# A fused sparse attention and MLP kernel: instruction order from a scheduling model with DMA limits as traced

## The chip, the cores and the metric

The kernel runs on one core of one Trainium2 chip. The metric is the device time of one execution in microseconds (us), as the median of several runs. The profile is of one execution. Its engines are PE (TensorE), ACT (ScalarE), DVE (VectorE), POOL (GpSimd) and SP (SyncE, which here issues transfers only); PEld is TensorE's weight load.

## What is computed

Attention over 4 batches, 8 heads, 768 positions and a head size of 64, in which each query sees only 6 of 24 chunks of 32 keys; then an MLP with an ELU over the 3072 resulting rows. The reference, cut to what matters:

```python
# q, k, v: (4, 8, 768, 64) float32; chunk = 32; top_k = 6; scale = 1/sqrt(64)
k_min, k_max = k_chunks.min(axis=3), k_chunks.max(axis=3)          # per chunk of 32 keys
ub = sum_d maximum(q * k_min, q * k_max)                           # bound per query and chunk
ub = where(causal, ub, -1e9)
top_chunks = argsort(ub)[..., -top_k:]
scores = scale * q @ k.T, masked to the chosen chunks and to earlier positions
attn = softmax(scores)
x = (attn @ v) as (3072, 512)
h = x @ w_in                                                       # w_in (512, 2048)
g = where(h > 0, h, exp(minimum(h, 0)) - 1)                        # ELU
out = g @ w_out                                                    # w_out (2048, 512)
```

## The kernel before

The kernel is written as a graph of operations. Each names the engines that could do it with a cost on each, the buffers that it reads and writes, and a priority. When the program is built, a simulated run of this graph on the five engines decides which engine does what and in which order, and which of a class's buffers each operation gets. The instructions are then emitted in that order. On the chip each engine works through its own fixed list, so an instruction whose data is late holds up all that stand behind it on its engine. The costs in the graph are used only for building; nothing of the model runs on the chip.

The work is cut into eight parts i = (b, h): batch b and half h of 384 positions. Each part has four head pairs r. For each pair, `prep` loads K, Q and V, transposes K and Q on PE and forms the chunk bounds; `select` makes the mask for two pairs; `attend` does scores, exponentials, attention times V, and the transposed result `xt`. `mlp(i)` needs the four `xt` of its part.

The parameters, which a search has set (numbers of buffers per class, gates of the weight loads, and offsets of priorities):

```python
T = dict(kf=6, qf=5, vf=7, pt=12, xt=12, gT=26, qt=3, qr=3, rhs=5, nfirst=2, vlate=4.17,
         gate=[1, 2, 3, 4, 5, 5, 8, 11], attw=[10.3, 19.0], mlp=[14.0, 15.1], loada=18.12,
         prepa=9.74, sela=2.41, fill=50)
```

The transfers in the model: each of the three queues (SP, ACT, POOL) works at one transfer at a time, and the queues that are busy share the bandwidth equally.

```python
def run(self, at=None, dma_lat=(700.0, 1300.0)):
    ...
    rings = {e: [] for e in (SP, ACT, POOL)}
    ...
    def transfer(t):
        ...
            live = [r for r in rings.values() if r and r[0][0] <= dma_at]
            ...
            if live:
                stop = min(stop, dma_at + min(r[0][1] for r in live) * len(live))
                for r in live:
                    r[0][1] -= (stop - dma_at) / len(live)
            ...
                    o.finish = dma_at + dma_lat[1]
```

The loads of a pair: two heads each of K, Q and V, 96 KB per transfer, in runs of 256 bytes (64 float32 of one position). All go on SP's queue but four Q loads at the start. Those of the first `nfirst` pairs come before everything else; V is later than K and Q by `vlate` in priority.

```python
for buf, src, late in ((kf, k, 0.0), (qf, q, 0.001), (vf, v, T["vlate"])):
    for hd in range(2):
        early = first and src is not v
        dma(..., (-100.0 + r) if early else prio + late, 450.0, ..., eng=ACT if early and late else SP)   # L411
```

The weights: four parts each of `w_in` and `w_out`, converted from float32 to bfloat16 in the transfer, issued by POOL. Each may be issued only once a certain number of V tiles has been cast to bfloat16 on POOL (L522); those numbers are `gate`.

```python
g.op(f"w_in{i}", c_dma(POOL, 900.0),
     lambda e: nc.gpsimd.dma_start(out=w_in_sb[:, :, 512 * i:512 * (i + 1)], in_=...),      # L364; w_out: L371
     writes=[(fixed, ("wi", i))], prio=-1.0, xfer=3400.0,
     after=[casts[W_GATE[i] - 1]] if W_GATE[i] else [])
```

TensorE's work by lines of the kernel: L454 transposes K and Q (float32, three blocks each); L540 multiplies queries with the chunk bounds; L606 scores; L662 attention times V; L687 transposes the result; L704 the first product of the MLP (per chunk fc four matmuls of 384 columns); L731 the second (per token tile tt and quarter c four matmuls of 512 columns):

```python
for fc in range(NFC):                       # 16
    pr = mlp_prio(i, 0.6 * fc / NFC)
    ... h: 4 matmuls (PE), e: exp (ACT, L712), m: e - 1 (POOL, L716), gT: min(max(h, 0), m) (DVE, L720)
for tt in range(3):
    for c in range(4):
        pr = mlp_prio(i, 0.6 + 0.4 * (tt * 4 + c) / 12)
        ... reads gts[4c : 4c + 4]
    ... copy to SBUF (L739), store
```

One tile `gT` holds one chunk fc of a part, so a part needs 16 of them until its last token tile has read them. Matmuls on zeros fill TensorE where the model has it idle, at the lowest priority:

```python
last = None
for i in range(T["fill"]):
    def fill(e, bank=bank):
        for _ in range(2):
            nc.tensor.matmul(ap(bank), lhsT=zeros[:, 0:P], rhs=zeros, start=True, stop=True)   # L762
    last = g.op("fill", {PE: (432, 600)}, fill, writes=[(bank, 0)], prio=1e6,
                after=[last] if last else [])
```

Of the kernel before, what the change touches and what calls it, by code (L numbers as in the profile page):

```python
# [29 lines left out]
NFC = DFF // P  # L30
# [7 lines left out]
SEM = 45.0  # L38


T = dict(kf=6, qf=5, vf=7, pt=12, xt=12, gT=26, qt=3, qr=3, rhs=5, nfirst=2, vlate=4.17,
         gate=[1, 2, 3, 4, 5, 5, 8, 11], attw=[10.3, 19.0], mlp=[14.0, 15.1], loada=18.12,
         prepa=9.74, sela=2.41, fill=50)


class Buf:
# [19 lines left out]
class Graph:  # L66
# [38 lines left out]
        self.ops.append(o)  # L105
        return o

    def run(self, at=None, dma_lat=(700.0, 1300.0)):
        free = {n: [(0.0, s) for s in range(len(v))] for n, v in self.slots.items()}
        engines = (PE, ACT, DVE, POOL, SP)  # L110
        at = {e: (at or {}).get(e, 0.0) for e in engines}
# [1 line left out]
        events = sorted({0.0, *at.values()})  # L113
        arriving = []
        rings = {e: [] for e in (SP, ACT, POOL)}
        dma_at, asked = 0.0, -1.0
        port_free = {DVE: 0.0, POOL: 0.0}
        for o in self.ops:
# [24 lines left out]
        def transfer(t):  # L143
            nonlocal dma_at, asked
            if asked <= t:
                asked = -1.0
            while True:
                live = [r for r in rings.values() if r and r[0][0] <= dma_at]
                later = [r[0][0] for r in rings.values() if r and r[0][0] > dma_at]
                stop = min([t] + later)  # L150
                if live:
                    stop = min(stop, dma_at + min(r[0][1] for r in live) * len(live))
                    for r in live:
                        r[0][1] -= (stop - dma_at) / len(live)
                dma_at = stop
                for r in live:
                    if r[0][1] <= 1e-6:
                        o = r.pop(0)[2]
                        o.finish = dma_at + dma_lat[1]
                        settle(o)  # L160
                if dma_at >= t:
                    break
            live = [r for r in rings.values() if r]
            if live:
                due = max(t, min(r[0][0] for r in live)) + min(r[0][1] for r in live) + 1.0
                if not due - 40.0 < asked <= due + 40.0:
                    asked = due
                    heapq.heappush(events, due)

        while left or any(rings.values()):  # L170
            if not events:
                held = {n: len(v) for n, v in free.items()}
                stuck = [o.name for e in engines for _, _, o in avail[e]][:40]
                raise RuntimeError(f"stuck: {left} left, free {held}, {stuck}")
            t = heapq.heappop(events)
            while events and events[0] <= t:
                heapq.heappop(events)
            transfer(t)
            while arriving and arriving[0][0] <= t:
                _, _, o = heapq.heappop(arriving)  # L180
                for e in o.engines:
                    bisect.insort(avail[e], (o.prio, o.seq, o))
            moved = True
            while moved:
                moved = False
                for e in engines:
                    if at[e] > t:
                        continue
                    lst = avail[e]
                    pick = None  # L190
                    i = 0
                    while i < len(lst):
                        o = lst[i][2]
                        if o.start is not None:
                            lst.pop(i)
                            continue
                        ok = True
                        for b in o.bufs:
                            if b.slot is None:
                                if not any(ft <= t for ft, _ in free[b.cls]):  # L200
                                    ok = False
                                    break
                            elif b.cls == "bank" and any(x != e and ft > t for x, ft in b.used.items()):
                                ok = False
                                break
                        if ok:
                            pick = o
                            lst.pop(i)
                            break
                        i += 1  # L210
                    if pick is None:
                        continue
                    o = pick
                    dur, lat = o.engines[e]
                    o.engine, o.start = e, t
                    if e == POOL or (e == DVE and o.port):
                        held = max(0.0, port_free[DVE if e == POOL else POOL] - t)
                        dur, lat = dur + held, lat + held
                        port_free[e] = t + dur
                    at[e] = t + dur  # L220
                    heapq.heappush(events, at[e])
                    for b in o.bufs:
                        if b.slot is None:
                            fl = free[b.cls]
                            k = min((ft, s, j) for j, (ft, s) in enumerate(fl) if ft <= t)[2]
                            b.slot = fl.pop(k)[1]
                    if o.xfer is None:
                        o.finish = t + lat
                        settle(o)
                    else:  # L230
                        rings[e].append([t + dur + dma_lat[0], o.xfer, o])
                        heapq.heappush(events, t + dur + dma_lat[0] + o.xfer)
                    order.append(o)
                    left -= 1
                    moved = True
# [30 lines left out]
def kernel(  # L266
# [95 lines left out]
    def load_w_in(i):  # L362
        g.op(f"w_in{i}", c_dma(POOL, 900.0),
             lambda e: nc.gpsimd.dma_start(out=w_in_sb[:, :, 512 * i:512 * (i + 1)],  # L364
                                           in_=wi[:, :, 512 * i:512 * (i + 1)]),
             writes=[(fixed, ("wi", i))], prio=-1.0, xfer=3400.0,
             after=[casts[W_GATE[i] - 1]] if W_GATE[i] else [])

    def load_w_out(i):
        g.op(f"w_out{i}", c_dma(POOL, 900.0),  # L370
             lambda e: nc.gpsimd.dma_start(out=w_out_sb[:, 4 * i:4 * i + 4, :],  # L371
                                           in_=wo[:, 4 * i:4 * i + 4, :]),
             writes=[(fixed, ("wo", i))], prio=-1.0, xfer=3400.0,
             after=[casts[W_GATE[4 + i] - 1]] if W_GATE[4 + i] else [])


# [28 lines left out]
    g.op("table", {ACT: (1300, 1300)}, lambda e: nc.scalar.activation(out=warm, in_=warm, func=AF.Exp),  # L405
         prio=-90.0)

    def dma(dst_src, writes, reads, prio, xfer, name, eng=SP, issue=490.0):
        def emit(e):
            d, s_ = dst_src()  # L410
            (nc.scalar if e == ACT else nc.sync).dma_start(out=d, in_=s_)  # L411
# [15 lines left out]
    def prep(b, h, r, prio):  # L427
        kf, qf, vf = load(b, h, r, prio - LOADAHEAD)
        tag = f"{b}{h}{r}"
        if h == 0:  # L430
# [3 lines left out]
            if b < 2:  # L434
                def ec(e, lb=lb):
# [4 lines left out]
                    else:  # L440
# [1 line left out]
                            out=ap(lb)[hi].rearrange("p h s -> p (h s)"),  # L442
                            in_=econst[hi].rearrange("p h c w -> p (h c w)"))
                g.op("ec" + tag, {DVE: (480, 560)}, ec, writes=[(lb, "e")], port=True,
                     prio=prio + 0.5, after=[ecs[-2]] if len(ecs) > 1 else [])
        lb = lhs[b, r]
        rb = rhs[b, h, r] = g.buf(f"rhs{h}")
        kst = ks[b, r]
# [33 lines left out]
        put("kt", lambda: ap(kt), lambda: ap(bank)[:, 0:HS], c_both(HS), [(bank, 0)], [(kt, 0)], prio)  # L482
        for hd, rows in enumerate((lo, hi)):
            put("ka", lambda hd=hd: ap(lb)[lo, hd, ts], lambda rows=rows: ap(kt)[rows],
                {DVE: (175, 260), POOL: (500, 560)}, [(kt, 0)], [(lb, (h, hd))], prio + 0.5)

        def sub(e):
            eng = nc.vector if e == DVE else nc.gpsimd
# [26 lines left out]
             reads=[(qt, 0)], writes=[(qr, 0)], prio=prio, port=True)  # L515
        for hd, rows in enumerate((lo, hi)):
            put("qa", lambda hd=hd: ap(rb)[lo, hd], lambda rows=rows: ap(qt)[rows],
                {DVE: (275, 360), POOL: (500, 560), ACT: (386, 480)}, [(qt, 0)], [(rb, hd)], prio + 0.5)

        casts.append(g.op(  # L520
            "v" + tag, {POOL: (520, 580)},
# [68 lines left out]
    def attend(b, h, r, prio, w):  # L590
# [2 lines left out]
        ls, rs = lhs[b, r], rhs[b, h, r]  # L593
        nst = len(steps[h])
        for si, segs in enumerate(steps[h]):
            pr = prio + w * 0.8 * si / nst
            wtot = max(pc + wd for (_k, _c, wd, pc) in segs)
            pt = g.buf("pt")
            both = wtot <= 256
# [47 lines left out]
                     port=True)  # L647
            for (kb, c0, wd, pc) in segs:
                seg[kb] = (pt, pc - (c0 - HS * h))
        pr = prio + w * 0.8  # L650
        o3 = g.buf("bank")

        def o3v():
# [41 lines left out]
    def mlp(i):  # L695
        b, h = divmod(i, 2)
        gts = []
        for fc in range(NFC):
            pr = mlp_prio(i, 0.6 * fc / NFC)
            bank = g.buf("bank")  # L700

            def mm1(e, bank=bank, fc=fc):
# [21 lines left out]
        for tt in range(3):  # L724
            bank, ob = g.buf("bank"), g.buf("o")
            for c in range(4):
                pr = mlp_prio(i, 0.6 + 0.4 * (tt * 4 + c) / 12)

                def mm2(e, bank=bank, c=c, tt=tt):
                    for fc in range(4 * c, 4 * c + 4):  # L730
# [16 lines left out]
    for i in range(2 * B):  # L747
# [5 lines left out]
            select(b, h, gr, att_prio(i, 0.5 * gr) - PREPAHEAD + T["sela"])  # L753
        for r in range(NPAIR):
            attend(b, h, r, att_prio(i, 0.25 * r), 0.25 * w)
    last = None
    for i in range(T["fill"]):
        bank = g.buf("bank")

        def fill(e, bank=bank):  # L760
            for _ in range(2):
                nc.tensor.matmul(ap(bank), lhsT=zeros[:, 0:P], rhs=zeros, start=True, stop=True)  # L762
        last = g.op("fill", {PE: (432, 600)}, fill, writes=[(bank, 0)], prio=1e6,
                    after=[last] if last else [])
    for i in range(4):
        load_w_in(i)
    for i in range(4):
# [40 lines left out]
```

## Time and profile before

| | before |
|---|---|
| median of 3 runs | 309.26 us (306.78 to 311.76) |
| span of the profiled execution | 308.6 us, clock 0.994 |
| read from memory, written | 27.26 MB, 6.29 MB |
| transfers on SP's queue | 64 of K, 60 of Q, 64 of V, 24 stores |
| transfers on POOL's queue | 4 of w_in, 4 of w_out, 512 KB each as written |

How to read it: busy time is the time in which an engine has at least one instruction running, as a share of the span. Strips have 40 slices of 7.7 us, each digit the busy share in tenths. The chain of waits is followed back from the last instruction; what stands on it sets the end. A timeline's line gives start, duration, engine, line, operation, what it writes and reads, how many; in brackets the idle time of the engine before it, and what ended that. Matmuls overlap in the profile, so their single durations add up to more than the time they take; the step from one to the next is what counts. A line number is that of the kernel before.

### The profile page before, as it was taken

How to read it: one execution, taken by the hardware profiler on the slowest of the kernel's cores; microseconds unless marked ns; L12 is line 12 of the kernel's file. 1: busy time of each engine (PE TensorE's matmuls, PEld its weight loads, DVE VectorE, ACT ScalarE, POOL GpSimd, SP SyncE). 2: the span in 40 equal slices, each digit the busy share in tenths (PEclk: the TensorE clock that was granted, in tenths of full speed). 3: DMA queues.
4: the chain of work that ended last, by engine and by line, in shares of the span. 5: the costliest groups of instructions: out<-in, count | busy, mean ns of one | idle time of the engine just before them, and what ended most of it. 6: DMA issues, size and time to landing. Idle time of an engine off the chain costs nothing.

```text
span 308.6 us, 6957 instructions
## 1 busy us (share of the span) xinstructions
PE 295.0 (96%) x2346; PEld 178.3 (58%) x2372; DVE 221.6 (72%) x676; ACT 204.2 (66%) x449; POOL 143.5 (46%) x309
## 2 busy tenths in 40 slices
PE   8965599999999999999999999999999999999998
PEld 3533355666566555765665565765665556655643
DVE  8953748998789947986799846894889649722820
ACT  2843328996599466967587748995698668853720
POOL 7845335675368414763466214661266124411710
PEclk9999979999999999999999999999999999999999
DMA  8999979979876514223332222230100010001002
GB/s 168 170 212 216 190 170 167 186 172 183 197 211 140 118 72 111 51 53 87 85 88 51 54 93 62 52 80 34 70 1 2 0 70 35 2 34 51 20 2 102
DMA packets 84515, 29.82 MB, mean 97 GB/s; under 512 B 77312, under 2 KB 81408, under 8 KB 84480
## 3 DMA queue, kind: packets, MB, share of 16 engines
q1 hardware_dynamic: 78656, 24.79, 33.1%
q0 software_dynamic: 4224, 4.19, 8.9%
q10 hardware_dynamic: 1600, 0.39, 0.6%
q8 instruction: 19, 0.31, 0.4%
q14 instruction: 16, 0.13, 0.2%
HBM read 27.26 MB, written 6.29 MB: 109 GB/s over the span
## 4 chain that ended last, share of the span: by engine, by line
PE 87%; DMA 7%; SPq 5%; issue 1%
PE bank L704 27%; PE bank L731 26%; PE bank L606 11%; PE bank L662 7%; PE bank L454 6%; PE bank L540 6%; SPq L411 5%; DMA qf<-in_q_dram 4%; DMA kf<-in_k_dram 3%; PE bank L762 2%; PE bank L687 2%
## 5 line engine op out<-in xcount | busy, mean ns | idle before, releaser
L704 PE MATMUL bank<-xt,w_in_sb 128*128 128x384 bf16 x512 | 95.8, 326 | 0.0
L716 POOL TENSOR_SCALAR m<-e 128x384 f32<-128x384 f32 x128 | 66.3, 524 | 58.2 <-ACT e L712 49.1
L731 PE MATMUL bank<-w_out_sb,gT 128*128 128x512 bf16 x362 | 92.0, 379 | 1.2 <-issue 0.2
L618 ACT ACTIVATE pt<-bank 128x384 bf16<-128x384 f32 (+1 forms) x160 | 76.6, 538 | 18.3 <-PE bank L606 18.0
L720 DVE SCALAR_TENSOR_TENSOR gT<-bank,m 128x384 bf16<-128x384 f32 x128 | 68.3, 547 | 13.1 <-POOL m L716 11.5
L712 ACT ACTIVATE e<-bank 128x384 f32<-128x384 f32 x128 | 61.8, 503 | 12.0 <-PE bank L704 9.8
L704 PEld LDWEIGHTS <-w_in_sb 128*128 128x128 bf16 x512 | 48.7, 98 | 28.6 <-issue 0.6
L464 POOL COPY lhs<-kt 64x384 bf16<-64x384 bf16 x62 | 32.7, 527 | 60.1 <-ACT kt L460 58.1
L731 PEld LDWEIGHTS <-gT 128*128 128x128 bf16 x384 | 35.9, 98 | 32.5 <-issue 0.6
L606 PE MATMUL bank<-rhs,lhs 128*128 128x384 bf16 (+2 forms) x288 | 54.4, 290 | 0.1
L606 PEld LDWEIGHTS <-lhs 128*128 128x128 bf16 x288 | 25.8, 98 | 19.0 <-issue 1.7
L474 DVE TENSOR_REDUCE kmm<-bank 128x12 f32<-128x384 f32 x64 | 33.2, 544 | 1.4 <-ACT kt L460 1.2
L739 ACT ACTIVATE o<-bank 128x512 f32<-128x512 f32 x23 | 13.7, 595 | 30.5 <-PE bank L731 28.9
L460 ACT ACTIVATE kt<-bank 128x384 bf16<-128x384 f32 x32 | 15.8, 494 | 23.6 <-PE bank L454 22.8
L460 ACT ACTIVATE rhs<-qt 64x384 bf16<-64x384 f32 x51 | 26.7, 523 | 4.3 <-DVE qt L462 3.5
L662 PEld LDWEIGHTS <-pt 128*128 128x128 bf16 x672 | 24.6, 99 | 8.1 <-issue 4.7
L762 PE MATMUL bank<-zeros 128*128 128x512 bf16 x96 | 26.9, 410 | 1.4 <-DVE warm L336 1.3
L633 DVE TENSOR_TENSOR pt<-pt,tri 128x512 bf16<-128x512 bf16 x32 | 15.4, 481 | 17.5 <-ACT pt L618 17.4
L662 PE MATMUL bank<-vext,pt 128*128 128x65 bf16 x672 | 26.6, 195 | 0.0
L454 PE MATMUL bank<-ident_f,kf 128*128 128x128 f32 x96 | 15.9, 274 | 6.0 <-DMA kf<-in_k_dram 6.0
L522 POOL TENSOR_SCALAR vext<-vf 128x384 bf16<-128x384 f32 x32 | 17.2, 543 | 8.6 <-DMA vf<-in_v_dram 4.0
L624 ACT ACTIVATE pt<-bank 128x512 bf16<-128x512 f32 x32 | 19.5, 609 | 1.9 <-PE bank L606 1.9
(55 smaller groups left out, 268.5 us busy)
## 6 DMA issues: line engine op xcount, KB each, us to landing
kf<-in_k_dram SPq DMA_DIRECT2D x64, 96.0 KB, 2.5
vf<-in_v_dram SPq DMA_DIRECT2D x64, 96.0 KB, 2.8
out_dram<-o SPq DMA_DIRECT2D x24, 256.0 KB, 2.0
qf<-in_q_dram SPq DMA_DIRECT2D x60, 96.0 KB, 2.5
w_in_sb<-in_moe_w_in_dram POOLq DMA_DIRECT2D x4, 512.0 KB, 8.2
w_out_sb<-in_moe_w_out_dram POOLq DMA_DIRECT2D x4, 512.0 KB, 7.7
qf<-in_q_dram ACTq DMA_DIRECT2D x4, 96.0 KB, 3.5
```

What stands on the lines that cost most here:

```text
L454: nc.tensor.transpose(ap(bk)[:, P * n:P * (n + 1)], ap(src)[:, n], ident_f)
L460: nc.scalar.activation(out=dst(), in_=src(), func=AF.Copy)
L474: nc.vector.tensor_reduce(out=ap(kmm)[:, w, :], in_=ap(bank)[:, 0:HS].rearrange("p (c w) -> p c w", w=CHUNK), axis=AX.X, op=op)
L606: nc.tensor.matmul(ap(banks[hd])[:, o + pc:o + pc + wd], lhsT=ap(ls)[:, hd, P * kb:P * (kb + 1)], rhs=ap(rs)[:, hd, c0 - HS * h:c0 - HS * ...
L618: lambda e, hd=hd, pt=pt, banks=banks, wtot=wtot: nc.scalar.activation(out=ap(pt)[:, hd, 0:wtot], in_=ap(banks[hd])[:, 0:wtot], func=AF.Ex ...
L662: nc.tensor.matmul(o3v()[:, hd, qi, :], lhsT=ap(pt)[:, hd, P * qi + off:P * qi + off + P], rhs=ap(vx[b, r])[:, kb, hd, :], start=(kb == 0) ...
L704: nc.tensor.matmul(ap(bank)[:, 0:HS], lhsT=w_in_sb[:, kk, P * fc:P * (fc + 1)], rhs=ap(xT[b, h, kk]), start=(kk == 0), stop=(kk == NKK - 1))
L712: lambda e, eb=eb, bank=bank: nc.scalar.activation(out=ap(eb), in_=ap(bank)[:, 0:HS], func=AF.Exp),
L716: lambda e, eb=eb, mb=mb: nc.gpsimd.tensor_scalar(out=ap(mb), in0=ap(eb), scalar1=-1.0, scalar2=1.0, op0=AOT.add, op1=AOT.mult),
L720: lambda e, gt=gt, bank=bank, mb=mb: nc.vector.scalar_tensor_tensor(out=ap(gt), in0=ap(bank)[:, 0:HS], scalar=0.0, in1=ap(mb), op0=AOT.max ...
L731: nc.tensor.matmul(ap(bank), lhsT=ap(gts[fc])[:, P * tt:P * (tt + 1)], rhs=w_out_sb[:, fc, :], start=(fc == 0), stop=(fc == NFC - 1))
L762: nc.tensor.matmul(ap(bank), lhsT=zeros[:, 0:P], rhs=zeros, start=True, stop=True)
```

## The change

The scheduling model is altered to follow the transfers as they were traced, and the parameters are set anew by a search in the altered model. The computation is the same. What is altered:

- POOL's queue (weights) has seven times the share of the other queues when several are busy.
- SP and ACT together issue no load or store in the model while eight of theirs are under way.
- A transfer lands 900 instead of 1300 ns after its last byte; a weight part takes 3200 instead of 3400 ns; an issue on SP costs 530 instead of 490 ns.
- Filler matmuls: the first `cold` pairs cost 860 ns, and a pair depends on the one before the last instead of on the last.
- The offsets of some priorities (copies after a transpose, the split of the MLP's priorities, the attention's) become parameters.

The diff's core:

```diff
-T = dict(kf=6, qf=5, vf=7, pt=12, xt=12, gT=26, qt=3, qr=3, rhs=5, nfirst=2, vlate=4.17,
-         gate=[1, 2, 3, 4, 5, 5, 8, 11], attw=[10.3, 19.0], mlp=[14.0, 15.1], loada=18.12,
-         prepa=9.74, sela=2.41, fill=50)
+T = dict(kf=4, qf=9, vf=2, pt=9, xt=9, gT=17, qt=5, qr=16, rhs=3, nfirst=2, vlate=6.25,
+         gate=[2, 2, 5, 6, 6, 7, 8, 10], attw=[9.57, 19.03], mlp=[13.31, 15.5], loada=0.26,
+         prepa=10.36, sela=0.01, fill=40, cold=6, evo=0.13, mf=0.3, sf=0.5)
...
-    def run(self, at=None, dma_lat=(700.0, 1300.0)):
+    def run(self, at=None, dma_lat=(700.0, 900.0)):
...
+        share = {SP: 1.0, ACT: 1.0, POOL: 7.0}
+        flying = [0, 0]
...
-                live = [r for r in rings.values() if r and r[0][0] <= dma_at]
+                live = [(r, share[e]) for e, r in rings.items() if r and r[0][0] <= dma_at]
+                total = sum(w for _, w in live)
...
-                    stop = min(stop, dma_at + min(r[0][1] for r in live) * len(live))
-                    for r in live:
-                        r[0][1] -= (stop - dma_at) / len(live)
+                    stop = min(stop, dma_at + min(r[0][1] / w for r, w in live) * total)
+                    for r, w in live:
+                        r[0][1] -= (stop - dma_at) * w / total
...
-                        ok = True
-                        for b in o.bufs:
+                        ok = o.xfer is None or e == POOL or flying[1] < 8
+                        for b in o.bufs if ok else ():
...
-             writes=[(fixed, ("wi", i))], prio=-1.0, xfer=3400.0,
+             writes=[(fixed, ("wi", i))], prio=-1.0, xfer=3200.0,
...
-                {DVE: (175, 260), POOL: (500, 560)}, [(kt, 0)], [(lb, (h, hd))], prio + 0.5)
+                {DVE: (175, 260), POOL: (500, 560)}, [(kt, 0)], [(lb, (h, hd))], prio + T["evo"])
...
-            pr = prio + w * 0.8 * si / nst
+            pr = prio + w * T["sf"] * si / nst
...
-            pr = mlp_prio(i, 0.6 * fc / NFC)
+            pr = mlp_prio(i, T["mf"] * fc / NFC)
...
-        last = g.op("fill", {PE: (432, 600)}, fill, writes=[(bank, 0)], prio=1e6,
-                    after=[last] if last else [])
+        cost = 860 if i < T["cold"] else 432
+        last = g.op("fill", {PE: (cost, cost + 170)}, fill, writes=[(bank, 0)], prio=1e6,
+                    after=[fills[-2]] if len(fills) > 1 else [])
```

## The prediction, made before the change was run

> **What bounds the kernel now.** I read the page first, then the busy time of each engine in stretches, the chain of waits, and last the timelines of TensorE and GpSimd over the first 47 us. From the page:
>
> ```profile
> PE 295.0 (96%) x2346; PEld 178.3 (58%) x2372; DVE 221.6 (72%) x676; ACT 204.2 (66%) x449; POOL 143.5 (46%) x309
> ...
> PEclk9999979999999999999999999999999999999999
> DMA  8999979979876514223332222230100010001002
> ...
> PE 87%; DMA 7%; SPq 5%; issue 1%
> ```
>
> TensorE looks full, but its 295.0 us contain the filler matmuls on a tile of zeros (L762), which compute nothing. The same view of busy time by stretch, kept to L762 (columns: window, its length, PE busy and count, clock, DMA share, GB/s):
>
> ```profile
> 0.00:47.00 47.00, 22.18 (x78) 0.96 1.02 188
> 47.00:309.00 262.00, 4.76 (x20) 1.00 0.33 80
> ```
>
> Fillers take 22.18 of the first 47 us. For L704, the MLP's first product, the same view has no matmul there (its first starts at 48.8). So I worked out TensorE's real work from steady pieces of the chain: 128 groups of four L704 at 0.65 us = 83.2; 96 groups of four L731 at 0.86 = 82.6; 86,016 columns of scores at L704's rate (384 columns in 0.163 us) = 36.4; 672 matmuls of attention times V at 0.032 (30 in 0.91 to 1.02) = 21.5; 192 fp32 transposes at 0.11 (six in 0.66) = 21.1; chunk bounds, per batch twice 0.80 and twice 1.44, = 17.9; the last transposes 1.7% of the chain = 5.2. Sum **267.9 us**; the span is 308.6, so **40.7 us** are lost. Before 47 us the counts of the windows are 24 scores (2.6), 48 of L662 (1.5), 48 of L454 (5.3), 24 of L540 (3.0), 12 of L687 (0.65): 13.1 us of work, so **33.9 us are lost there** and only 6.8 in the 261.6 us after.
>
> What TensorE stands on, from its timeline (last column: idle before, and what ended it):
>
> ```profile
> 18.30 0.52 PE L454 MATMUL bank<-ident_f,kf 128*128 128x128 f32 x3 [2.92 <-DMA kf<-in_k_dram]
> ...
> 27.89 0.52 PE L454 MATMUL bank<-ident_f,kf 128*128 128x128 f32 x3 [3.07 <-DMA kf<-in_k_dram]
> ...
> 38.80 0.52 PE L454 MATMUL bank<-ident_f,qf 128*128 128x128 f32 x3 [3.90 <-DMA qf<-in_q_dram]
> ...
> 40.58 1.50 PE L540 MATMUL bank<-qr,kst 128*64 128x384 f32 x4
> 42.01 1.50 PE L662 MATMUL bank<-vext,pt 128*128 128x65 bf16 x24
> ```
>
> The three gaps end with a load of K or Q for the *second* half of batch 0. The 24 L662 at 42.01 are the last two head pairs of the *first* half, all that MLP tile 0 still lacks. GpSimd cast the fourth V tile at 23.03, so they could have run some 18 us earlier, but they stand in TensorE's fixed order behind the transposes that wait for loads. And the loads are late because of this, from GpSimd's timeline:
>
> ```profile
> 10.73 0.98 POOL L364 DMA_DIRECT2D w_in_sb<-in_moe_w_in_dram  x1
> ...
> 13.81 0.81 POOL L364 DMA_DIRECT2D w_in_sb<-in_moe_w_in_dram  x1
> ...
> 16.31 0.80 POOL L364 DMA_DIRECT2D w_in_sb<-in_moe_w_in_dram  x1
> ...
> 23.49 0.93 POOL L364 DMA_DIRECT2D w_in_sb<-in_moe_w_in_dram  x1
> ...
> 27.67 1.57 POOL L371 DMA_DIRECT2D w_out_sb<-in_moe_w_out_dram  x2
> ```
>
> Each group of weight issues lies ahead of a gap. K loads land after a median of 2.5 us, but at worst 9.3 (from the answer for the K tile; Q 10.1, V 11.3):
>
> ```profile
> DMA to landing us min/median/max: 1.9/2.5/9.3
> ```
>
> **What the Trainium skill says.** "DMA: Bandwidth & Descriptors", section "Queues, rings and completion order": each DMA engine takes turns between the queues it has work for, a whole packet at a time. The queue with the larger packets so gets the larger share. The trace agrees in kind: the load queue moved 24.79 MB in 78,656 packets (315 bytes each), the weight queue 4.19 MB written in 4,224 (993 bytes, from fp32 sources twice as large), and loads beside weights landed four times later than the median. The share of 7 against 1 is the change's own number; no view here measures it. "TensorE: Matmul & The Clock Gate", section "Part 1: The HAM clock gate": an idle window of about 3.4 us halves the clock. The trace fits: after the idle 3.90 us the 24 L662 took 1.50 us, while twelve took 0.53 at 30.53, and the clock of 40 to 50 us is 0.83. The fillers exist to avoid this, so they cost nothing while TensorE would wait anyway.
>
> **The change part by part.** No instruction of the computation is added or removed except ten filler pairs; order, buffers and gates move.
>
> 1. *The model of transfers* (weights 7 to 1 ahead of loads, eight loads in flight, landing 900 instead of 1300 ns): costs nothing at run time. The old model shared equally, so it took the second half's K and Q to arrive early and put their transposes ahead of the finished first half. The new one should place the L662 of pairs 2 and 3 ahead of them. The first half needs 24 loads at 0.51 us an issue on SyncE (1.02 for two) = 12 us, so issue ends near 15 with V late; with weights beside it the last V lands near 20 to 22 and its cast (0.5) is near the 23.0 of before. PV, normalise, transpose and copy took 42.0 to 46.4, partly cold: some 3.5 us. MLP tile 0 can then start near **27 us** instead of 48.8.
> 2. *Weight gates* from 1,2,3,4,5,5,8,11 to 2,2,5,6,6,7,8,10: two parts of w_in early, the third only after the first V of the second half is cast. So 2 rather than 3 weight parts compete with loads before some 24 us. L704 has 5.2 us of work on the first two parts (eight groups of 0.65), and a part took 8.2 us to land, so a third asked for near 25 is there at about 33, just when it is wanted.
> 3. *Sum at the start.* By 27 us TensorE can do the first half's attention (scores 2.6 + PV 1.5 + transposes 2.6 + bounds 1.6 + last transposes 0.65 = 9.0) and about 1 us more: 17 lost. From there to 47 us it has 10.4 of L704 and the second half's attention (about 16) on hand, against 20 us of time, but the loads must still arrive behind weights; I put 5 lost. Together **22 instead of 33.9: -12 us**.
> 4. *Fillers* 50 to 40 pairs, the first six modelled cold (twelve matmuls took 5.10 us here, 0.85 a pair). At the tail, pairs stand among the last useful matmuls:
>
> ```profile
> 302.33 0.59 PE L762 MATMUL bank<-zeros 128*128 128x512 bf16 x2
> 302.54 0.75 PEld L731 LDWEIGHTS <-gT 128*128 128x128 bf16 x4
> 302.76 1.03 PE L731 MATMUL bank<-w_out_sb,gT 128*128 128x512 bf16 x4
> ```
>
>    Three pairs at 301.03, 302.33 and 303.62 push the last product back by 3 x 0.43 = 1.3 us. With 34 warm pairs (14.7 us) and six cold (5.1), a start that wastes 22 us uses most of them up: **-1 us**.
> 5. *Buffers.* kf 4, vf 2, pt 9, xt 9, gT 17, rhs 3 are tighter; qf, qt, qr larger. gT 17 leaves one spare while a tile needs 16, so the next tile's products can scarcely be stored before the third token tile of the second product begins to free them. The model plans for this with its fixed durations; every departure becomes a wait. Mean DVE share is already 7.15 of 10 us. I put **+2 us**.
> 6. *Priorities* (mf 0.3, sf 0.5, evo, loada 0.26): the first product is drawn forward, PV too. In the middle TensorE is within some 2 us of full, so there is nothing to win there: 0.
>
> Sum: -12 - 1 + 2 = **-11 us, 309.3 to 298.3**.
>
> **The rivals.**
> A. *The loss moves and doesn't shrink.* The DMA engines are at 0.87 to 1.20 of their share over the first 40 us, and the two halves of batch 0 with all weights are many bytes; if transfers are the real bound there, another order only swaps which are late. For: those shares, and 168 to 216 GB/s throughout. Against: the finished half waited 18 us with its data landed, which no bandwidth forces. It would make 304 to 309.
> B. *Tight buffers bring new waits in the middle.* For: gT 17 and rhs 3, and a DVE at 95 to 99% in single stretches. Against: the kernel before, ordered in the same manner, loses under 3 us there. Each of seven tile changes costing 1.5 us would give back 10: about 306 to 308, or with A even 312.
> C. *Everything fits*: the fixed order is filled from 15 us on, and only latency and the first bytes are lost, some 15 us: 290.
> D. *Two V buffers block SyncE's single queue* (loads wait behind a V load whose buffer isn't cast yet), and the later loads come late: the start would keep 28 of its 34 us, about 303.
>
> **Range and chances.** C sets the low end, A and B together the high end: 289 to 308, with 298.3 in the middle. The 2% line is 303.1. The main step rests on a wait that is plainly an error of order, so I give 0.73 to faster, 0.20 to within 2% (A, D or B eating the gain), 0.07 to slower.
>
> **What would show it.** Right: the first L704 before 32 us; L662 of the first half ahead of the long DMA gaps; waits of L454 on DMA under 6 us in all instead of 9.9; useful work by 47 us of 23 or more; hardly any L762 after 290. Step 5 is wrong if TensorE's idle time between 50 and 300 us exceeds 5 us, with ACT, DVE or GpSimd's gT and m named. The prediction is wrong if the first L704 stays past 40, or if it comes early and then starves on w_in parts or on the second half.

## The result, and the profile after

| | before | after |
|---|---|---|
| median | 310.51 us (306.78 to 314.03) | 298.19 us (297.77 to 302.81) |
| ratio, 95% interval | | 0.9676 (0.958 to 0.9772) |
| span of the profiled execution | 308.6 | 296.7 |
| TensorE idle on loads of K and Q (L454, after: L459) | 9.9 | 0.4 |
| first matmul of the MLP (L704, after: L709) | 48.8 | 36.4 |
| useful work of TensorE before 47 us | 13.1 | 25.6 |
| lost before 47 us, lost from there to the last useful matmul, tail | 33.9, 3.1, 3.7 | 21.4, 3.7, 3.7 |

Executions over 1.5% slower than the fastest of their kernel are left out of the ratios; by the ratio the gain is 3.2%, about 10 us, where the medians and the profiled spans differ by 12. Useful work is worked out as in the prediction, from the counts of each line before 47 us and the same steady durations; "lost" is the rest. In the changed kernel's listing TensorE's lines stand five lower: L459 transposes of K and Q, L545 bounds, L611 scores, L667 attention times V, L692 last transposes, L709 and L736 the MLP, L767 fillers. The page of after, in the lines that answer to those shown of before:

```profile
PE 290.8 (98%) x2352; PEld 175.7 (59%) x2352; DVE 219.8 (74%) x669; ACT 205.0 (69%) x446; POOL 145.1 (49%) x317
...
PEclk9999999999999999999999999999999999999999
DMA  8899999998684662255421202121100001001002
...
PE 83%; DMA 8%; DVE 6%; SPq 1%; issue 0%; ACTq 0%; ACT 0%; POOL 0%
```

The two strips of before and after differ in little but the clock, which no longer drops between 40 and 50 us. What changed is in the answer on TensorE's waits (who waited for whom: total, times, longest):

```profile
PE bank L767 <- DVE warm L341: 1.3, 1, 1.3
PE bank L736 <- DMA w_out_sb<-in_moe_w_out_dram: 1.0, 1, 1.0
PE bank L611 <- ACT pt L623: 0.5, 1, 0.5
PE bank L459 <- DMA kf<-in_k_dram: 0.2, 1, 0.2
PE bank L459 <- DMA qf<-in_q_dram: 0.2, 1, 0.2
```

The loads of K and Q beside weights did not get faster. The answer for the K tile in the changed kernel:

```profile
DMA to landing us min/median/max: 2.0/2.6/11.1
```

The worst is later than the 9.3 of before (for Q 10.6 against 10.1; for V it fell from 11.3 to 7.9). Two things are different. The loads of K and Q for the first two pairs of the second half are now issued from 10.23 to 14.94, ahead of the first weight part (15.20), and land within 2.7 us; so the first two K tiles of that half are transposed at 13.53 and 16.37, instead of at 18.30 and 27.89. And where a load is still late, finished work no longer stands behind it. TensorE's timeline:

```profile
13.53 0.52 PE L459 MATMUL bank<-ident_f,kf 128*128 128x128 f32 x3
...
16.37 0.49 PE L459 MATMUL bank<-ident_f,kf 128*128 128x128 f32 x3
...
20.15 4.09 PE L767 MATMUL bank<-zeros 128*128 128x512 bf16 x18
24.08 0.53 PE L667 MATMUL bank<-vext,pt 128*128 128x65 bf16 x12
...
26.52 0.52 PE L459 MATMUL bank<-ident_f,kf 128*128 128x128 f32 x3 [0.23 <-DMA kf<-in_k_dram]
...
29.18 0.89 PE L667 MATMUL bank<-vext,pt 128*128 128x65 bf16 x24
```

Fillers fill the stretch in which the load is under way, the first half's attention times V stands *ahead* of the transposes that wait for the load, and its last 24 come at 29.18 instead of 42.01. The weights are issued later too (GpSimd's timeline):

```profile
15.20 1.75 POOL L369 DMA_DIRECT2D w_in_sb<-in_moe_w_in_dram  x2
...
30.09 0.83 POOL L369 DMA_DIRECT2D w_in_sb<-in_moe_w_in_dram  x1
...
32.79 0.80 POOL L369 DMA_DIRECT2D w_in_sb<-in_moe_w_in_dram  x1
33.59 0.75 POOL L376 DMA_DIRECT2D w_out_sb<-in_moe_w_out_dram  x1
```

By 30 us before had asked for six parts, two of them parts of w_out that no matmul read until 67.5 us; after has asked for two.

### The profile page after: what moved, and what is told of

It reads as the page before. It is cut to its first block, busy times and chain, and to the rows that moved or that the text cites. A ratio compares the mean times of both kernels' runs of the same rounds, so it can differ in the third digit from the quotient of the medians.

```text
span 296.7 us, 6941 instructions
## 1 busy us (share of the span) xinstructions
PE 290.8 (98%) x2352; PEld 175.7 (59%) x2352; DVE 219.8 (74%) x669; ACT 205.0 (69%) x446; POOL 145.1 (49%) x317
## 4 chain that ended last, share of the span: by engine, by line
PE 83%; DMA 8%; DVE 6%; SPq 1%; issue 0%; ACTq 0%; ACT 0%; POOL 0%
PE bank L709 26%; PE bank L736 26%; PE bank L611 10%; PE bank L667 6%; PE bank L459 6%; PE bank L545 6%; DMA kf<-in_k_dram 3%; DMA w_out_sb<-in_moe_w_out_dram 3%; PE bank L767 3%; DMA qf<-in_q_dram 2%; DVE gT L725 2%; PE bank L692 2%; SPq L416 1%; DVE pt L638 1%; DVE lhs L442 1%; DVE kmm L479 1%
## 5 line engine op out<-in xcount | busy, mean ns | idle before, releaser
L736 PE MATMUL bank<-w_out_sb,gT 128*128 128x512 bf16 x384 | 95.3, 379 | 1.0 <-DMA w_out_sb<-in_moe_w_out_dram 1.0
L709 PE MATMUL bank<-xt,w_in_sb 128*128 128x384 bf16 x512 | 92.0, 326 | 0.0
L623 ACT ACTIVATE pt<-bank 128x384 bf16<-128x384 f32 (+1 forms) x160 | 74.7, 532 | 17.6 <-PE bank L611 16.9
L709 PEld LDWEIGHTS <-w_in_sb 128*128 128x128 bf16 x512 | 48.9, 98 | 31.0 <-issue 1.2
L736 PEld LDWEIGHTS <-gT 128*128 128x128 bf16 x384 | 36.6, 98 | 33.6 <-issue 1.3
L611 PE MATMUL bank<-rhs,lhs 128*128 128x384 bf16 (+2 forms) x288 | 51.7, 290 | 0.5 <-ACT pt L623 0.5
L469 POOL COPY lhs<-kt 64x384 bf16<-64x384 bf16 x58 | 30.1, 520 | 31.0 <-ACT kt L465 28.0
L611 PEld LDWEIGHTS <-lhs 128*128 128x128 bf16 x288 | 25.1, 98 | 18.1 <-issue 3.1
L667 PEld LDWEIGHTS <-pt 128*128 128x128 bf16 x672 | 24.2, 97 | 6.5 <-issue 2.0
L744 ACT ACTIVATE o<-bank 128x512 f32<-128x512 f32 x20 | 11.9, 595 | 22.6 <-PE bank L736 22.6
L527 POOL TENSOR_SCALAR vext<-vf 128x384 bf16<-128x384 f32 x32 | 17.5, 549 | 20.1 <-DMA vf<-in_v_dram 16.3
L465 ACT ACTIVATE rhs<-qt 64x384 bf16<-64x384 f32 x48 | 25.1, 522 | 2.4 <-DVE qt L467 1.5
L667 PE MATMUL bank<-vext,pt 128*128 128x65 bf16 x672 | 26.0, 193 | 0.0
L767 PE MATMUL bank<-zeros 128*128 128x512 bf16 x80 | 22.7, 410 | 1.3 <-DVE warm L341 1.3
L465 ACT ACTIVATE kt<-bank 128x384 bf16<-128x384 f32 x28 | 13.6, 489 | 12.9 <-PE bank L459 12.4
L465 ACT ACTIVATE qt<-bank 128x384 f32<-128x384 f32 x28 | 13.7, 489 | 11.3 <-PE bank L459 11.3
```

What stands on the lines that cost most here:

```text
L465: nc.scalar.activation(out=dst(), in_=src(), func=AF.Copy)
L469: nc.gpsimd.tensor_copy(out=dst(), in_=src())
L611: nc.tensor.matmul(ap(banks[hd])[:, o + pc:o + pc + wd], lhsT=ap(ls)[:, hd, P * kb:P * (kb + 1)], rhs=ap(rs)[:, hd, c0 - HS * h:c0 - HS * ...
L623: lambda e, hd=hd, pt=pt, banks=banks, wtot=wtot: nc.scalar.activation(out=ap(pt)[:, hd, 0:wtot], in_=ap(banks[hd])[:, 0:wtot], func=AF.Ex ...
L667: nc.tensor.matmul(o3v()[:, hd, qi, :], lhsT=ap(pt)[:, hd, P * qi + off:P * qi + off + P], rhs=ap(vx[b, r])[:, kb, hd, :], start=(kb == 0) ...
L709: nc.tensor.matmul(ap(bank)[:, 0:HS], lhsT=w_in_sb[:, kk, P * fc:P * (fc + 1)], rhs=ap(xT[b, h, kk]), start=(kk == 0), stop=(kk == NKK - 1))
```

## The experiments

Theory: the truer model of the transfers brings the gain, because the order no longer stands in front of late loads. Rivals: the new parameters bring it, above all the gates that hold the weights back; or the transfers are the bound, and any order only moves the loss. Each kernel is ordered by its own model run; ratios are to the kernel before. "Gaps" is TensorE's idle time before L454 (or L459) on loads, "first" the first matmul of the MLP, "lost" what TensorE lost in the first 80 us. These three are read from one profiled execution of each kernel.

| | ratio, 95% interval | gaps | first | lost |
|---|---|---|---|---|
| before | 1 | 9.9 | 48.8 | 34.4 |
| after | 0.9676 (0.958 to 0.9772) | 0.4 | 36.4 | 21.7 |
| old parameters, new model | 0.9995 (0.9966 to 1.0024) | 0 | 40.8 | 29.3 |
| new parameters, old model | 0.9871 (0.9824 to 0.9917) | 3.6 | 43.0 | 28.8 |
| after, old gates | 0.9766 (0.9716 to 0.9816) | 1.0 | 38.7 | 25.3 |
| before, new gates | 0.9888 (0.9838 to 0.9938) | 4.5 | 43.2 | 27.9 |
| before, a quarter of the weights | 0.9686 (0.9638 to 0.9735) | 0.8 | 38.4 | 23.0 |
| after, a quarter of the weights | 0.9605 (0.9545 to 0.9664) | 0.2 | 36.2 | 20.2 |
| after, equal shares | 1.0004 (0.9978 to 1.0031) | 6.2 | 48.0 | 34.1 |
| after, no limit of eight | 0.9753 (0.9682 to 0.9823) | 4.6 | 42.6 | 28.0 |
| before, longer source runs | 1.0019 (0.9984 to 1.0053) | 6.4 | 46.8 | 32.1 |
| after, old buffers | 0.9788 (0.9713 to 0.9863) | 0.2 | 36.4 | 23.1 |
| after, no tail fillers | 0.9598 (0.955 to 0.9647) | 0.8 | 36.8 | 21.8 |
| searched anew | 0.9666 (0.9601 to 0.973) | 1.9 | 36.3 | 21.3 |

### Model or parameters

```diff
# the changed kernel with the parameters of before
-T = dict(kf=4, qf=9, vf=2, ...)
+T = dict(kf=6, qf=5, vf=7, ..., fill=50, cold=6, evo=0.5, mf=0.6, sf=0.8)
```

> The parameters of before (buffers, gates, priorities), ordered by the new model of transfers and fillers. If the truer model is what brings the gain by itself (my theory: the old order stands in front of loads that come late), the three gaps of L454 on DMA (9.9 us in all) shrink to under 3 us and the time falls to 299 to 302. If the parameters bring it, the time stays at 306 to 310. If the weights' early gates really starve the loads, no order can mend it, the gaps turn into fillers, and the time stays at 304 to 308 without DMA gaps.

308.97 us, ratio 0.9995: no gain. My theory in its plain form falls. The gaps did close, but became fillers (busy time in windows, of L767 alone, in this kernel):

```profile
0.00:47.00 47.00, 26.16 (x100) 1.00 1.01 189
47.00:80.00 33.00, 0.00 (x0) 1.00 0.90 187
```

All 100 filler matmuls run in the first 47 us, against 78 before. The order knows that the loads are late and has nothing to put in their place. It gains 5.1 us before 80 us by the table, and in this trace new waits on DVE (1.6 us at 79.40, 1.64 at 89.97) return a part; the time shows none of it.

```diff
# the changed kernel with the old model
-    def run(self, at=None, dma_lat=(700.0, 900.0)):
+    def run(self, at=None, dma_lat=(700.0, 1300.0)):
-        share = {SP: 1.0, ACT: 1.0, POOL: 7.0}
+        share = {SP: 1.0, ACT: 1.0, POOL: 1.0}
-   ... flying[1] < 8 ... xfer=3200.0 ... issue=530.0 ... cost = 860 if ... after=[fills[-2]]
+   ... flying[1] < 999 ... xfer=3400.0 ... issue=490.0 ... cost = 432 ... after=[fills[-1]]
```

> The new parameters, ordered by the old model (equal shares, no limit of eight, landing 1300 ns, warm fillers). Theory (model): the order is again wrong about the loads, 305 to 309. Rival (parameters, above all the later gates of the weights): nearly all of the gain stays, 297 to 300.

306.37 us, ratio 0.9871: some 4 of the 10 us. Gaps of 3.6 us are back, and the clock of 20 to 30 us is 0.66. So the two halves are worth nothing and 1.3% alone and 3.2% together.

### What in the model counts

```diff
-        share = {SP: 1.0, ACT: 1.0, POOL: 7.0}
+        share = {SP: 1.0, ACT: 1.0, POOL: 1.0}
```

> The changed kernel with one thing undone: the model shares the bandwidth equally instead of 7 to 1. Theory now (model and parameters only pay together): gaps of L454 on DMA of 3 to 5 us come back, 301 to 305. Rival (the share is of no matter, the rest of the parameters does it): 297 to 299.

308.45 us, ratio 1.0004: **one number of the model takes back the whole gain**, more than I expected. The gates are those of after, and the first two weight parts are issued at 14.68, as in after at 15.20. Only the order differs. TensorE's timeline in the stretch shown above of after:

```profile
20.16 0.59 PE L767 MATMUL bank<-zeros 128*128 128x512 bf16 x2
26.41 0.88 PE L459 MATMUL bank<-ident_f,kf 128*128 128x128 f32 x3 [5.66 <-DMA kf<-in_k_dram]
27.08 3.62 PE L767 MATMUL bank<-zeros 128*128 128x512 bf16 x8
30.49 0.85 PE L459 MATMUL bank<-ident_f,qf 128*128 128x128 f32 x3
31.13 1.95 PE L767 MATMUL bank<-zeros 128*128 128x512 bf16 x6
32.92 0.53 PE L667 MATMUL bank<-vext,pt 128*128 128x65 bf16 x12
```

The same K tile is ready at the same time (26.41, in after 26.52), but here the twelve L667 stand behind it: 32.92 instead of 24.08. The two K tiles before it are transposed as early as in after (at 13.07 and 16.36), so early loads bring nothing under this order. The gap also cools TensorE: eight fillers take 3.62 us, where eighteen took 4.09. That is the half clock after an idle window of the Trainium skill ("TensorE: Matmul & The Clock Gate", "Part 1: The HAM clock gate"), and the trace agrees. This is the mechanism of the prediction's first step, shown by one edit.

```diff
-                        ok = o.xfer is None or e == POOL or flying[1] < 8
+                        ok = o.xfer is None or e == POOL or flying[1] < 999
```

> The changed kernel without the limit of eight loads in flight in the model. The order near the start should hardly differ, since SyncE issues every 0.51 us and a load lands after 2.6, five in flight; 297 to 299. If the limit is what makes the plan true, gaps or waits of 3 us and more, 301 to 304.

301.64 us, ratio 0.9753; its runs (300.61 to 304.51) lie above 297.77 to 298.44 of after, though the intervals of the two ratios overlap. I expected no difference. The trace is of the slowest of these runs (304.51). In it TensorE waits at a Q transpose, ahead of the last transposes of the first half's result:

```profile
37.61 0.87 PE L459 MATMUL bank<-ident_f,qf 128*128 128x128 f32 x3 [3.62 <-DMA qf<-in_q_dram]
38.27 0.53 PE L692 MATMUL bank<-ident_b,on 128*128 128x128 bf16 x3
```

In after the same two stand in the same order (at 32.72 and 33.49), without a wait. So TensorE's order is not what differs here; the load is late. SyncE's timeline, first of this kernel, then of after:

```profile
30.36 1.59 SPq L416 DMA_DIRECT2D qf<-in_q_dram  x2
...
29.50 1.02 SPq L416 DMA_DIRECT2D qf<-in_q_dram  x2
```

Here the two loads come with the third weight part (issued at 30.57) and land after 6.2 and 6.0 us; in after they are ahead of it (30.09) and land after 2.5 and 2.3. They have the same place in SyncE's list in both kernels, so this trace doesn't show what the limit itself is worth.

The median of 2.6 us misled me all the same: beside weights even the issues take longer. In after two K issues take 3.69 us from 19.54 on, where two took 0.95 at 10.23.

### Gates and buffers

```diff
# the changed kernel with the old gates       # and the reverse, before with the new gates
-gate=[2, 2, 5, 6, 6, 7, 8, 10]               -gate=[1, 2, 3, 4, 5, 5, 8, 11]
+gate=[1, 2, 3, 4, 5, 5, 8, 11]               +gate=[2, 2, 5, 6, 6, 7, 8, 10]
```

> The changed kernel with the gates of before (weights 1,2,3,4,5,5,8,11) and nothing else. Theory (model): the order follows the late loads, 299 to 302. Rival (gates): weights compete with the loads of the second half again, 304 to 308.

302.92 us, ratio 0.9766: between both theories, nearer to mine. With the loads late again the order keeps the gaps small (1.0 us) and pays with fillers: all 80 run at the start.

> The kernel before with the new gates (2,2,5,6,6,7,8,10), old model and all other parameters of before. Theory (model): little, 305 to 309. Rival (gates): the loads of the second half come earlier by themselves, the DMA gaps of TensorE fall under 4 us, 299 to 303.

306.55 us, ratio 0.9888. The gaps fall to 4.5 us by the gates alone. Part of the gain is hidden: this kernel has 50 filler pairs, uses fewer of them at the start, and the rest run at its end.

```profile
298.27 1.03 PE L736 MATMUL bank<-w_out_sb,gT 128*128 128x512 bf16 x4
...
299.13 4.91 PE L767 MATMUL bank<-zeros 128*128 128x512 bf16 x22
```

The tail after the last useful matmul is 5.8 instead of 3.7 us: 2.1 us of zeros.

```diff
-T = dict(kf=4, qf=9, vf=2, pt=9, xt=9, gT=17, qt=5, qr=16, rhs=3, ...)
+T = dict(kf=6, qf=5, vf=7, pt=12, xt=12, gT=26, qt=3, qr=3, rhs=5, ...)
```

> The changed kernel with the numbers of buffers of before (kf 6, qf 5, vf 7, pt 12, xt 12, gT 26, qt 3, qr 3, rhs 5), everything else new. If the tight new buffers only cost (my step 5, measured at some 1 us in the middle), 296 to 298. If they are part of what makes the order good, because the parameters were searched together, 300 to 305.

302.1 us, ratio 0.9788. The old, mostly larger numbers look slower (the interval overlaps that of after), though no wait on DMA comes back (0.2 us). The third weight part is issued at 24.87 instead of 30.09 and lost time rises by 1.4 us before 80 us. The profiled run explains 2 us of the difference (span 298.7 against 296.7); what the rest is stays open, and so does which buffer matters.

### The weights as cause

```diff
-  dma_start(out=w_in_sb[:, :, 512 * i:512 * (i + 1)], in_=wi[:, :, 512 * i:512 * (i + 1)])
+  dma_start(out=w_in_sb[:, :, 512 * i:512 * i + P],   in_=wi[:, :, 512 * i:512 * i + P])
-  lhsT=w_in_sb[:, kk, P * fc:P * (fc + 1)]
+  lhsT=w_in_sb[:, kk, 512 * (fc // 4):512 * (fc // 4) + P]        # w_out likewise
```

Both kernels leave out three quarters of the weights and use the rest four times; the engines' instructions are the same.

> The kernel before, same order, but each of the eight weight transfers carries a quarter of its bytes, and the products use that quarter four times over (so the output isn't the reference's; the instructions of the engines are the same in number and size). If weights taking the DMA engines from the loads are what TensorE's three gaps are made of, the 9.9 us of gaps on DMA fall under 3 us, the clock stays full at 40 to 50 us, and the time falls by 8 to 12 us to about 298 to 301. If the loads are late for another reason (256-byte runs, issue rate on one queue), the gaps stay above 7 us and the time above 305.

300.04 us, ratio 0.9686, as expected: the order of before loses nearly all its gaps (0.8 us left), because the loads land in time. The answer for its K tile:

```profile
DMA to landing us min/median/max: 2.0/2.6/5.0
```

So the weights were what made the loads late, and fewer bytes of them alone bring as much as the whole change (0.9686 against 0.9676).

> The changed kernel with the same cut of the weights' bytes to a quarter. Its order is planned around the weights, so where TensorE would wait there are fillers or work: if so only its 1.0 us wait on w_out and a little more goes, 295 to 298. If weights still cost it time that the order only hides, it falls under 293.

297.33 us, ratio 0.9605: about 1 us below after. The changed order has little left to win from lighter weights; it still loses 20.2 us before 80, and runs its 70 fillers there.

```diff
# before; the transposes write every third column, so that K and Q keep their order
-  src[b, 2 * r + hd, ts].rearrange("(n p) d -> p n d", p=P)
+  src[b, 2 * r + hd, ts].rearrange("(n p) d -> p n d" if src is v else "(p n) d -> p n d", p=P)
-  nc.tensor.transpose(ap(bk)[:, P * n:P * (n + 1)], ap(src)[:, n], ident_f)
+  nc.tensor.transpose(ap(bk)[:, n:HS:3], ap(src)[:, n], ident_f)
```

> The kernel before, same order, with K and Q loaded in runs of 768 bytes instead of 256 (each partition takes three neighbouring positions, and the fp32 transposes write every third column, which restores the order). If the queues are served packet by packet, longer packets give the loads a larger share beside the weights, and fewer bytes of overhead: the worst K and Q landings fall from 9.3 and 10.1 us to under 7, the gaps on DMA from 9.9 to under 6 us, and the time to 301 to 305. If the issue rate of the queue or the weights' bytes alone set the landing, nothing changes: 307 to 310.

310.63 us, ratio 1.0019, and it tells nothing of the question. (Its gaps are 6.4 us instead of 9.9 and its time is the same: gaps alone don't measure the gain.) The two heads lie interleaved in the tile, so the runs at the destination stayed at 256 bytes, and the packets did too:

```profile
DMA packets 84515, 29.82 MB, mean 97 GB/s; under 512 B 77312, under 2 KB 81408, under 8 KB 84480
```

That is the line of before to the last digit. Only the issues grew, two K issues from 1.02 to some 1.22 us. Whether longer load packets would take a larger share beside the weights was not tried; no run here shows what sets the share of a queue.

### The tail, and a better plan

```diff
         for o in order:
+            if o.name == "fill" and o.start > 100e3:
+                continue
             o.emit(o.engine)
```

> The changed kernel without its last five filler pairs (three stand among the last useful matmuls, two behind them). If the three pairs lie on the path that sets the end, 3 x 0.43 = 1.3 us go and the time falls to 296.6 to 297.2. If the last products wait for something else there, nothing changes (298).

297.14 us, ratio 0.9598, the lowest of this study, though the interval overlaps that of after. In the trace the last products now run through:

```profile
284.64 7.07 PE L736 MATMUL bank<-w_out_sb,gT 128*128 128x512 bf16 x32
...
291.75 0.60 ACT L744 ACTIVATE o<-bank 128x512 f32<-128x512 f32 x1 [2.86 <-PE bank L736]
```

The last copy starts at 291.75 instead of 293.24: 1.5 us, the three pairs and a little. What those matmuls were spaced for exists only in the model.

```diff
-T = dict(kf=4, qf=9, vf=2, pt=9, xt=9, gT=17, qt=5, qr=16, rhs=3, vlate=6.25, gate=[2, 2, 5, 6, 6, 7, 8, 10], ...)
+T = dict(kf=2, qf=5, vf=3, pt=8, xt=10, gT=18, qt=5, qr=14, rhs=2, vlate=17.56, gate=[1, 2, 3, 4, 5, 5, 7, 11], ...)
```

> The new model, its parameters searched anew (gates 1,2,3,4,5,5,7,11 again, but V so late that the weights are issued as late as in the changed kernel: planned at 15, 20, 28, 31, 40, 41, 52, 61 us), and no filler pairs at the end. Its plan ends 1.9 us before that of the changed kernel. If the model is now true enough that a better plan is a better kernel, the time falls below that of the changed kernel without tail fillers by some 1 to 2 us, to 295 to 296.5. If the plan's last microseconds are noise, or the tighter buffers (kf 2, rhs 2) turn departures into waits, 298 to 303.

297.82 us, ratio 0.9666: no better than the changed kernel without tail fillers. Its start is as good (21.3 us lost before 80), but TensorE waits again for w_out and for loads:

```profile
PE bank L734 <- DMA w_out_sb<-in_moe_w_out_dram: 1.1, 1, 1.1
PE bank L457 <- DMA qf<-in_q_dram: 1.0, 2, 0.8
PE bank L457 <- DMA kf<-in_k_dram: 0.9, 2, 0.6
```

These waits are 3.0 us, against 1.0 in the changed kernel without tail fillers: the planned 1.9 us are lost in departures of that size. Two quite different sets of parameters, both searched in the new model, end at the same level. Of the first five weight parts three are issued at nearly the same times (15.3, 29.5 and 32.3 us here; 15.2, 30.1 and 32.8 in after), the other two later (20.7 and 41.7 instead of 16.2 and 33.6). The gate numbers look like those of before, but V, which they count, is cast later.

## Why the prediction was right, point by point

The time and the cause in kind were right: 298.3 against 298.19, by an order that no longer stands behind late loads. Equal shares alone (ratio 1.0004) show it. That the figures meet so closely is partly luck: in the two profiled executions the terms are -12.5, 0 and +0.6 instead of -12, -1 and +2, so two misses nearly cancel.

- **Start, -12 us.** Measured 33.9 to 21.4 = -12.5. But the path was another: the first L709 came at 36.4, not near 27. The step that failed is "PV, normalise, transpose and copy, some 3.5 us after the last V cast". That cast came at 23.11, as estimated (four of the 24 loads are issued by ACT and not by SyncE, which did not show there), but the first half's pairs 2 and 3 still had their selection to do. DVE's timeline in after: the mask copy, the triangle before the last V products, and the two result copies:

```profile
22.80 0.54 DVE L585 COPY rhs<-selT 64x384 bf16<-64x384 bf16 x2
...
28.45 0.29 DVE L647 TENSOR_TENSOR pt<-pt,tri 128x256 bf16<-128x256 bf16 x1
...
33.78 0.62 DVE L697 COPY xt<-bank 128x384 bf16<-128x384 bf16 x2
```

  Scores, exponentials and triangle stand between the first and the second, normalising behind DVE's work for the second half between the second and the third. My 18 us of waiting in before had the same fault: it counted from the V cast alone. There the scores of pairs 2 and 3 themselves stood behind the wait that ended at 27.89, and their last mask was done at 36.00, so the 24 L662 waited 6 us with all their inputs there (DVE's timeline of before):

```profile
35.65 0.35 DVE L642 TENSOR_TENSOR pt<-pt,tri 128x256 bf16<-128x256 bf16 x1
```

  What I had not counted on made up for it: TensorE used the time for the second half and the next batch (54 transposes and 32 bound matmuls by 47 us, before 48 and 24, and 22 scores of the second half).
- **Gates.** Held back as predicted, the third part at 30.09 rather than 25. That the model pays only together with new parameters I did not see; my text let it act alone, and with the old parameters it gave nothing. Of the new parameters the gates alone are worth 1.1% in the old model (0.9888), and without them the rest keeps 2.3% (0.9766).
- **Fillers, -1 us.** Failed: the same three pairs still stand in the tail. The size was right, as taking them away showed 1.5 us.
- **Buffers, +2 us.** Lost time from 47 us to the last useful matmul rose from 3.1 to 3.7, part of it a wait on w_out of 1.0: the sign holds there, the size doesn't. With the old numbers the kernel looks slower, not faster, so they are no mere cost.
- **Priorities, 0.** Nothing contradicts it in the middle; alone it was not tried.

Rival A (transfers are the bound) fails: the same bytes, some 10 us less. Rival D's two V buffers do hold V up (GpSimd waits 16.3 us for V instead of 4.0), but with seven of them the kernel was no faster. Of the five signs named, the first L704 before 32 us and hardly any filler after 290 were wrong; L662 of the first half ahead of late loads, the waits under 6 us and the useful work over 23 were right.

What stays open: by the ratios, undoing the share, the gates, the buffers or the limit returns 10.2, 2.8, 3.5 and 2.4 us, together 19 of a gain of 10. The parts aren't additive, and the runs don't say how much of a single one is its own effect and how much the loss of a set that was searched as a whole. Nor was a new search in the old model tried, which would tell the truer model from mere further search.

## What to carry to other kernels

Where an engine's order is fixed in advance, ask of each wait not only why the data is late but what stands behind the waiting instruction: finished work behind it is the gain. A model that plans such an order has to know who is served first when queues compete, and its parameters have to be searched again once it does; a truer model with old parameters, or the reverse, may bring little or nothing. Fillers belong only where the trace, not the plan, shows an engine waiting.

## What was not expected of the hardware

Loads of K stayed as late as before (worst 11.1 us against 9.3) in a kernel that is some 10 us faster. Two issues on SyncE's queue took 3.69 us beside weight transfers instead of 0.95 us, so the issue is held up as well as the data: with a quarter of the weights' bytes the longest single issue of a K load fell from 3.2 to 1.6 us. And runs that are longer at the source alone left the packet count at 84,515.
